# Eight single PSUM banks in one pool, freely placed steps, and a new order and buffer plan for an attention + gated-FFN kernel

## Chip, cores, metric

One core of a Trainium2 chip (the experiments ran on four chips; every ratio is to the kernel before on the same chip). The metric is the device time of one execution in microseconds (us). Most executions of one kernel agree to within 0.3%. Engines: PE does matrix products and PE transposes (PEld is its weight load), DVE, ACT and POOL do elementwise work, SP issues the DMA transfers from one queue, in program order.

## The reference, cut to what matters

```python
# q, k, v: (8 batches, 8 heads, 576, 64)
q_s = softmax(q, axis=-1); k_s = softmax(k, axis=2)
kv  = einsum('bhsd,bhse->bhde', k_s, v)              # 64 x 64 per head
x   = einsum('bhsd,bhde->bhse', q_s, kv)              # -> 4608 tokens x 512
out = ((x @ w1) * (x @ w2)) @ w3 @ w_out              # d_ff = 1024
```

In the course of the run 38.8 MB come in from memory: the weights and, batch by batch, q, k and v.

## The kernel before

The kernel is a list of about 1350 small steps. A step has an engine, dependencies and buffers. Three lists made by a search are stored in the file: `ORDER` (the order in which all steps are emitted), `SLOTS` (which tile of its pool each buffer takes) and, in `ORDER`, filler matmuls on a blank tile that keep PE busy while it would wait. A step waits for whatever last used the tile that it writes.

```python
tiles("st", 8, [P, 2 * RK * D], F32)      # staging tiles: every load lands in one of them
tiles("ps", 6, [P, 512], F32, psum)       # six single PSUM banks
tiles("pa", 1, [P, 2, 512], F32, psum)    # one double bank: all kv, x and query transposes of batch 0
...
def load(key, nbytes, rate, view, src):   # all loads, transposes and stores: one SP queue
    b = buf("st")
    def emit():
        nc.sync.dma_start(out=view(b.tile), in_=src)
...
def xm(...):                              # x product: four 64x64 quadrants side by side
    for j in range(2):
        for t in range(2):
            nc.tensor.matmul(px.tile[64*t:64*t+64, j, 0:n], lhsT=kv2..., rhs=qsT..., ...)
def xc(...):                              # its eviction, both banks in one ACT instruction
    nc.scalar.copy(out=xt_buf[g].tile[:, 2*i:2*i+2, o:o+n], in_=px.tile[:, :, 0:n])
...
for n in order:                           # emission
    if isinstance(n, tuple): self.fill(self.pools[n[0]][n[1]], n[2])
    else:                    self.tasks[n].emit()
```

Per batch: exponentials (ACT), sums (DVE), normalised queries (POOL), their transposes (by PE for batch 0, by DMA for the rest), kv, x. The FFN is computed in six token groups; five of them use a Winograd-like scheme with seven product pairs per block, evictions to `uu` tiles, sums from PSUM on DVE and a last product on POOL. W3·W_out is formed first, from eight w3 loads and four w_out loads.

The softmax here doesn't subtract the row's maximum and nothing guards it: scores larger than these inputs give would overflow.

Of the kernel before, what the change touches and what calls it, by code (L numbers as in the profile page):

```python
# [15 lines left out]

ORDER = [
    ('ps', 2, 27), 10, 6, 11, 4, 2, 8, 0, 142, 144, 96, 145, 97, ('ps', 2, 29), 151, 153, 152, 3, 98, 88,
    80, 143, 1, 81, 14, 89, ('ps', 2, 9), 104, 72, 90, 5, 73, ('ps', 2, 12), 17, 146, 154, 147, 7, 74, 12,
    82, 105, ('ps', 2, 3), 69, 148, ('ps', 2, 10), 16, 149, 15, 68, 150, 99, 70, 83, 128, 155, 91, 13, 106,  # L20
    100, 156, 92, 71, 101, 129, 84, 137, 75, 140, 136, 157, 76, 27, 159, 77, 158, 9, 102, 130, 21, 85, 103,
    141, 20, 131, 160, 138, 93, 86, 139, 132, 87, 161, 120, 107, 162, 94, 214, 112, 24, 163, 133, 164, 19,
    108, 212, 121, 182, 113, 213, 18, 165, 26, 78, 114, 166, 109, 79, 181, 167, 110, 168, 122, 95, 134, 22,
    169, 23, 193, 123, 170, 29, 124, 111, 28, 171, 176, 125, 135, 25, 126, 172, 32, 115, 127, 175, 116,
    427, 117, 205, 430, 207, 424, 431, 208, 436, 432, 428, 206, 437, 177, 425, 438, 179, 118, 187, 426,
    433, 188, 178, 173, 31, 439, 209, 429, 30, 210, 442, 119, 35, 440, 34, 443, 441, 454, 444, 215, 457,
    202, 434, 211, 189, 194, 445, 435, 455, 185, 446, 199, 216, 183, 451, 236, 190, 460, 184, 238, 461,
    447, 204, 448, 174, 456, 239, 449, 462, 463, 237, 36, 450, 203, 464, 37, 200, 458, 195, 466, 201, 217,
    33, 459, 452, 467, 465, 469, 192, 468, 219, 230, 220, 197, 218, 233, 1099, 221, 470, 186, 222, 180,
    1113, 223, 453, 38, 1106, 234, 232, 41, 196, 224, 1107, 231, 1114, 240, 198, 225, 235, 1092, 43, 191,  # L30
    1108, 250, 241, 251, 243, 1115, 245, 252, 1093, 471, 226, 1094, 244, 227, 242, 1109, 228, 269, 246,
    1100, 229, 1095, 270, 1101, 267, 40, 472, 1116, 39, 1110, 247, 1102, 473, 42, 1096, 248, 482, 268, 48,
    476, 1103, 491, 477, 475, 493, 506, 1117, 480, 507, 271, 478, 474, 481, 272, 253, 249, 492, 510, 479,
    483, 263, 494, 495, 521, 484, 508, 496, 485, 486, 254, 47, 498, 487, 266, 488, 511, 44, 255, 509, 499,
    497, 273, 489, 256, 513, 501, 500, 490, 522, 512, 502, 514, 503, 525, 264, 265, 504, 527, 516, 515,
    526, 523, 261, 536, 517, 505, 528, 524, 262, 518, 551, 529, 519, 553, 46, 274, 281, 530, 520, 1105,
    282, 537, 275, 45, 552, 538, 49, 276, 540, 539, 555, 1118, 541, 533, 283, 556, 531, 1104, 534, 543, 52,
    257, 554, 544, 566, 535, 1112, 542, 277, 258, 558, 567, 300, 568, 545, 546, 559, 570, 304, 532, 548,
    547, 259, 571, 561, 549, 260, 557, 581, 550, 560, 298, 573, 1120, 278, 562, 582, 279, 563, 302, 569,
    284, 583, 564, 574, 585, 572, 586, 1121, 575, 285, 576, 296, 587, 565, 577, 280, 578, 297, 588, 303,  # L40
    286, 301, 1127, 589, 584, 287, 1128, 305, 591, 50, 288, 1134, 1119, 579, 289, 1135, 299, 1111, 306,
    590, 580, 316, 1097, 327, 592, 593, 53, 307, 328, 317, 1148, 311, 318, 1149, 594, 290, 1129, 291, 595,
    1122, 308, 309, 1150, 335, 310, 292, 1136, 293, 1130, 312, 1098, 1123, 1131, 54, 596, 1141, 1124, 1137,
    598, 294, 1126, 600, 313, 295, 597, 1125, 314, 1142, 333, 51, 615, 601, 334, 1143, 616, 617, 1138, 319,
    618, 619, 320, 315, 1144, 599, 620, 602, 331, 329, 336, 604, 622, 330, 603, 61, 621, 623, 55, 1151,
    605, 60, 624, 321, 625, 1152, 56, 337, 607, 58, 1145, 338, 626, 630, 1140, 608, 627, 631, 606, 628,
    342, 632, 647, 322, 629, 633, 634, 340, 609, 610, 635, 363, 323, 343, 651, 324, 645, 611, 612, 646,
    637, 613, 660, 638, 341, 325, 614, 636, 661, 649, 326, 639, 640, 332, 648, 347, 650, 642, 366, 641, 59,
    664, 364, 643, 1139, 652, 348, 1146, 365, 653, 339, 662, 665, 362, 654, 675, 359, 655, 663, 676, 667,
    644, 656, 657, 668, 344, 666, 349, 358, 345, 677, 658, 361, 679, 57, 669, 670, 360, 63, 690, 678, 680,  # L50
    378, 671, 659, 691, 346, 672, 367, 682, 681, 683, 673, 692, 1153, 684, 379, 674, 65, 694, 380, 66, 705,
    695, 693, 64, 687, 1154, 685, 688, 1147, 350, 697, 686, 351, 689, 707, 698, 696, 706, 354, 699, 700,
    355, 709, 708, 702, 710, 720, 739, 404, 712, 703, 740, 724, 721, 704, 711, 713, 1155, 725, 714, 715,
    402, 701, 743, 1156, 722, 744, 717, 373, 728, 718, 371, 352, 746, 716, 719, 729, 1157, 62, 368, 353,
    726, 372, 67, 741, 1133, 369, 727, 356, 731, 742, 730, 732, 754, 747, 733, 745, 755, 370, 734, 723,
    1158, 748, 758, 1159, 736, 735, 759, 751, 374, 389, 749, 769, 391, 752, 1169, 770, 375, 750, 753, 1170,
    357, 1171, 737, 773, 395, 738, 760, 381, 761, 396, 382, 1162, 393, 392, 756, 390, 1163, 757, 376, 1172,
    762, 383, 771, 763, 384, 764, 405, 774, 1164, 1173, 394, 766, 772, 377, 776, 397, 765, 775, 777, 398,
    1165, 784, 1160, 1166, 767, 409, 1132, 785, 778, 779, 1175, 768, 790, 1174, 403, 788, 781, 789, 410,
    786, 411, 791, 780, 1183, 792, 787, 1184, 1176, 793, 799, 399, 1177, 406, 782, 400, 800, 796, 1185,  # L60
    385, 803, 1178, 804, 794, 401, 1186, 795, 1179, 1187, 797, 814, 806, 1188, 815, 798, 816, 1161, 386,
    801, 1189, 807, 805, 407, 1180, 818, 808, 387, 1182, 819, 1190, 817, 811, 388, 802, 809, 783, 408,
    1191, 810, 1192, 1193, 812, 821, 1168, 820, 822, 412, 829, 823, 413, 824, 1197, 830, 825, 835, 1194,
    826, 1196, 833, 827, 1195, 1198, 1181, 418, 828, 1204, 419, 1205, 834, 844, 831, 813, 836, 832, 1199,
    837, 845, 1200, 1206, 838, 1201, 848, 846, 1207, 841, 847, 1208, 839, 842, 849, 1209, 850, 414, 843,
    863, 851, 415, 852, 840, 864, 1211, 853, 865, 416, 867, 866, 1212, 868, 855, 854, 856, 1213, 857, 878,
    1214, 860, 1215, 870, 861, 1217, 858, 871, 869, 1203, 859, 879, 1225, 1210, 893, 872, 1202, 1218, 1167,
    882, 1216, 875, 883, 873, 876, 894, 1226, 874, 885, 877, 897, 1227, 898, 862, 880, 1219, 881, 900,
    1220, 901, 1228, 417, 884, 886, 899, 1229, 903, 902, 1221, 1230, 887, 888, 1222, 908, 904, 890, 889,
    905, 923, 891, 910, 906, 909, 895, 1232, 924, 896, 1233, 911, 1234, 907, 912, 1239, 913, 892, 420,  # L70
    1235, 915, 914, 916, 1240, 421, 917, 927, 1236, 1241, 928, 920, 422, 1242, 921, 918, 922, 930, 919,
    938, 931, 925, 939, 933, 926, 1243, 929, 423, 942, 1244, 968, 940, 1238, 943, 932, 1246, 1231, 1247,
    934, 1237, 945, 941, 935, 953, 936, 1248, 954, 1249, 937, 946, 1253, 944, 1250, 955, 947, 948, 1251,
    957, 1224, 949, 972, 1245, 950, 958, 1254, 1252, 951, 960, 956, 959, 952, 961, 1260, 973, 962, 1261,
    963, 970, 965, 964, 1255, 969, 1262, 966, 976, 987, 1263, 977, 971, 967, 988, 1256, 1264, 979, 978,
    974, 980, 1267, 1257, 981, 991, 1268, 1258, 992, 982, 1223, 994, 984, 983, 1269, 1259, 975, 985, 993,
    1265, 1002, 989, 986, 1270, 1003, 1266, 995, 1274, 996, 1271, 990, 1006, 1275, 1007, 1008, 997, 1009,
    999, 998, 1276, 1010, 1000, 1019, 1011, 1012, 1001, 1277, 1013, 1017, 1014, 1278, 1032, 1281, 1018,
    1033, 1282, 1020, 1015, 1036, 1004, 1021, 1283, 1005, 1022, 1037, 1284, 1016, 1024, 1023, 1285, 1038,
    1039, 1288, 1287, 1040, 1025, 1289, 1041, 1280, 1026, 1042, 1027, 1279, 1034, 1043, 1029, 1028, 1044,  # L80
    1286, 1049, 1290, 1045, 1030, 1064, 1035, 1291, 1031, 1062, 1047, 1046, 1292, 1295, 1048, 1296, 1293,
    1050, 1051, 1273, 1302, 1052, 1294, 1063, 1303, 1065, 1053, 1054, 1066, 1304, 1055, 1056, 1305, 1067,
    1057, 1059, 1306, 1297, 1058, 1060, 1069, 1307, 1298, 1308, 1068, 1077, 1299, 1309, 1078, 1316, 1301,
# [81 lines left out]
def kernel(  # L165
# [11 lines left out]
    nc = tc.nc  # L177
# [524 lines left out]
```

## Time and profile before

| | before |
|---|---|
| median | 243.96 us (3 runs, 242.98 to 244.15) |
| PE / DVE / ACT / POOL busy in the profiled run | 228.0 / 155.7 / 146.2 / 96.0 us |
| first W3·W_out product starts | 18.95 us |
| last matmul ends, then tail | 238.7 us, 4.6 us |
| filler matmuls | 90 |

The page of the kernel before: busy time of each engine, then PE's busy tenths in 40 slices of the span, the clock that the throttle granted PE, and the DMA engines' share.

```profile
PE 228.0 (94%) x1876; PEld 114.5 (47%) x1876; DVE 155.7 (64%) x293; ACT 146.2 (60%) x280; POOL 96.0 (39%) x85
...
PE   8897889988799999999989999999999999999992
...
PEclk9999999999999999999999999999999999999999
DMA  6999999999999999998995906272151004244656
```

The table of windows has one stretch per line: busy time (and number of instructions) of PE, PEld, DVE, ACT, POOL, then the mean granted clock, the DMA share (as the profile counts it, it can exceed 1) and the GB/s moved.

```profile
10.00:20.00 10.00, 8.39 (x87) 6.29 (x85) 7.23 (x13) 2.09 (x2) 2.14 (x1) 1.00 1.00 357
20.00:30.00 10.00, 7.83 (x81) 3.61 (x79) 4.84 (x7) 2.42 (x4) 5.84 (x4) 1.00 0.96 348
60.00:70.00 10.00, 8.30 (x115) 3.79 (x115) 6.59 (x15) 5.89 (x11) 5.04 (x4) 1.00 1.14 321
...
90.00:100.00 10.00, 9.81 (x126) 4.22 (x124) 6.81 (x15) 7.69 (x16) 6.37 (x5) 1.00 1.20 278
100.00:110.00 10.00, 10.00 (x55) 4.16 (x54) 7.58 (x14) 9.58 (x18) 6.29 (x5) 1.00 1.08 364
...
130.00:230.00 100.00, 100.00 (x623) 48.42 (x621) 62.20 (x116) 54.83 (x112) 33.34 (x29) 1.00 0.39 84
```

So the kernel has three stages: a start that waits for weights, a long middle in which PE runs just behind the loads (the DMA share stays near 1 to 120 us), and from 130 us a stretch in which PE is never idle. What PE does inside "busy" needs the timeline (start, duration, engine, line, operation, tiles, count). This is a stretch of the last stage:

```profile
170.96 0.59 PE L550 MATMUL ps<-xt,wc 128*128 128x512 f16 x2
171.39 0.59 PE L550 MATMUL ps<-xt,w 128*128 128x512 f16 x2
171.91 0.28 PE L466 MATMUL pa<-qsT,kv 64*64 64x192 f16 x4
172.12 0.60 PE L550 MATMUL ps<-xt,w 128*128 128x512 f16 x2
```

A pair of 512-column matmuls starts every 0.43 us. From the pair at 171.39 to the one at 172.12 it is 0.73 us although the x product between them needs only about 0.08: the visit to the 64x64 products costs about 0.22 us more. It is no single case: of the 51 visits in this trace 42 have no recorded idle time of PE in them, and the median of their extra time is 0.22 us. The Trainium skill, "TensorEngine Tiling (Array Packing)", Key Properties, states that a change of tiling mode drains the TensorE; this trace agrees with it, and gives the size of the whole visit (it cannot tell a drain from the weight loads of the four quadrants).

### The profile page before, as it was taken

To read this page: it belongs to the slowest core of one execution; us is meant where nothing else is said; L and a number is where in the kernel's file an instruction comes from. 1 tells how busy PE (TensorE), PEld (TensorE's weight loads), DVE (VectorE), ACT (ScalarE), POOL (GpSimd) and SP (SyncE) were. 2 spreads that over 40 slices of the span, in tenths; PEclk is the share of its full clock that TensorE was granted. 3 is DMA by queue.
4 is the path that set the end of the run, shared out by engine and by line. 5 is a ranking of instruction groups with operands and counts; after the bars stand their busy time and mean duration, and the time that the engine had idled before them with its cause. 6 is when DMAs were issued, how large, how long until landed. Compare 5 with 4: busy or idle time off the path is not lost.

```text
span 243.3 us, 4956 instructions
## 1 busy us (share of the span) xinstructions
PE 228.0 (94%) x1876; PEld 114.5 (47%) x1876; DVE 155.7 (64%) x293; ACT 146.2 (60%) x280; POOL 96.0 (39%) x85
## 2 busy tenths in 40 slices
PE   8897889988799999999989999999999999999992
PEld 5673344434346654444434444444444444566650
DVE  1474435889588985778978977467664566654330
ACT  4310486886499988998759785455645453444430
POOL 2033510235648566574834492454103312312020
PEclk9999999999999999999999999999999999999999
DMA  6999999999999999998995906272151004244656
GB/s 228 399 355 347 340 363 358 377 390 252 282 376 288 339 392 300 313 334 286 247 290 202 239 20 137 51 154 65 24 113 40 1 22 108 45 108 89 139 117 134
DMA packets 41879, 52.68 MB, mean 217 GB/s; under 512 B 18816, under 2 KB 22912, under 8 KB 41856
## 3 DMA queue, kind: packets, MB, share of 16 engines
q1 hardware_dynamic: 41856, 52.37, 74.7%
q8 instruction: 14, 0.23, 0.4%
q14 instruction: 9, 0.07, 0.1%
HBM read 38.80 MB, written 9.44 MB: 198 GB/s over the span
## 4 chain that ended last, share of the span: by engine, by line
PE 56%; DMA 25%; ACT 6%; DVE 4%; POOL 3%; issue 2%; SPq 2%; ACTq 0%; DVEq 0%; POOLq 0%
PE ps L550 32%; PE ps L616 22%; DMA qsT<-eq 9%; DMA st<-in_q_dram 6%; DMA st<-in_moe_w_dram 4%; DMA st<-in_k_dram 3%; DMA st<-in_moe_w_out_dram 3%; POOL eq L390 3%; SPq L233 2%; PE pa L466 2%; ACT uu L571 2%; ACT eq L376 1%; ACT ek L355 1%; DVE cc L574 1%; ACT osb L626 1%
## 5 line engine op out<-in xcount | busy, mean ns | idle before, releaser
L574 DVE TENSOR_TENSOR cc<-ps,uu 128x512 f16<-128x512 f32 (+2 forms) x120 | 66.9, 577 | 36.9 <-PE ps L550 16.8
L571 ACT COPY uu<-ps 128x512 f32<-128x512 f32 (+2 forms) x120 | 57.3, 505 | 38.8 <-PE ps L550 34.9
L616 PE MATMUL ps<-W3O,ab 128*128 128x512 f16 x288 | 76.2, 380 | 0.0
L601 POOL TENSOR_TENSOR ab<-cc,cc 128x512 f16<-128x512 f16 (+2 forms) x40 | 39.1, 982 | 76.6 <-DVE cc L574 76.0
L550 PE MATMUL ps<-tt,wc 128*128 128x512 f16 (+2 forms) x240 | 56.6, 337 | 0.1
L390 POOL TENSOR_TENSOR eq<-eq,ds 128x1152 f16<-128x1152 f16 x16 | 34.8, 2173 | 34.8 <-DVE ds L387 16.7
L550 PEld LDWEIGHTS <-wc 128*128 128x128 f16 x320 | 29.5, 98 | 28.9 <-DVE tt L529 0.7
L550 PE MATMUL ps<-xt,w 128*128 128x512 f16 (+2 forms) x160 | 38.6, 337 | 0.3
L616 PEld LDWEIGHTS <-ab 128*128 128x128 f16 x288 | 26.6, 98 | 25.7
L380 DVE TENSOR_REDUCE ds<-eq 128x9 f32<-128x576 f16 x32 | 23.5, 744 | 16.5 <-ACT eq L376 16.4
L550 PEld LDWEIGHTS <-w 128*128 128x128 f16 x240 | 22.2, 98 | 20.0 <-issue 0.8
L355 ACT ACTIVATE ek<-st 128x576 f16<-128x576 f32 x32 | 20.6, 688 | 14.8 <-DMA st<-in_k_dram 14.8
L626 ACT ACTIVATE osb<-ps 128x512 f32<-128x512 f32 x35 | 20.7, 603 | 14.3 <-PE ps L616 13.5
L376 ACT ACTIVATE eq<-st 128x576 f16<-128x576 f32 x32 | 21.3, 686 | 11.5 <-DMA st<-in_q_dram 10.2
L574 DVE TENSOR_TENSOR ab<-ps,cc 128x512 f16<-128x512 f32 (+2 forms) x40 | 22.8, 576 | 6.6 <-PE ps L550 5.5
L473 ACT CAST xt<-pa 128x512 f16<-128x512 f32 (+4 forms) x38 | 21.5, 565 | 6.3 <-PE pa L466 6.1
L365 POOL CAST v<-st 128x1152 f16<-128x1152 f32 x16 | 19.0, 1190 | 14.0 <-DMA st<-in_v_dram 9.6
L550 PE MATMUL ps<-xt,wc 128*128 128x512 f16 (+2 forms) x80 | 20.3, 337 | 0.0
L550 PE MATMUL ps<-tt,w 128*128 128x512 f16 (+2 forms) x80 | 19.9, 337 | 0.0
L309 PE MATMUL ps<-ab,ab 128*128 128x512 f16 x64 | 16.2, 380 | 0.7 <-DVE ab L276 0.3
L494 PE MATMUL ps<-xt,w 128*128 128x512 f16 x64 | 14.8, 379 | 0.9 <-ACT cc L501 0.9
L668 PE MATMUL ps<-blank 128*128 128x256 f16 x90 | 13.6, 317 | 1.1 <-DVE blank L660 1.1
(41 smaller groups left out, 136.4 us busy)
## 6 DMA issues: line engine op xcount, KB each, us to landing
st<-in_q_dram SPq DMA_DIRECT2D x16, 576.0 KB, 6.7
st<-in_v_dram SPq DMA_DIRECT2D x16, 576.0 KB, 6.8
st<-in_k_dram SPq DMA_DIRECT2D x16, 576.0 KB, 8.1
out_dram<-osb SPq DMA_DIRECT2D x72, 128.0 KB, 2.4
st<-in_moe_w_dram SPq DMA_DIRECT2D x16, 512.0 KB, 7.4
st<-in_moe_w_out_dram SPq DMA_DIRECT2D x4, 512.0 KB, 6.8
qsT<-eq SPq DMA_TRANSPOSE x14, 5.8
```

The source lines that it names most:

```text
L355: nc.scalar.activation(out=ek.tile[:, :, j, :], func=AF.Exp, in_=vk(bk.tile)[:, j].rearrange("p (r d) -> p r d", r=RK))
L365: nc.gpsimd.tensor_copy(out=v16.tile[:, :, :, 0:D].rearrange("p r j d -> p j r d"), in_=vv(bv.tile).rearrange("p j (r d) -> p j r d", r=RK))
L376: nc.scalar.activation(out=eq.tile[:, :, j, :], func=AF.Exp, in_=vq(bq.tile)[:, j].rearrange("p (r d) -> p r d", r=RK))
L380: nc.vector.tensor_reduce(out=ds.tile[:, 0, j], axis=AX.X, op=ALU.add, in_=eq.tile[:, :, j, :])
L390: nc.gpsimd.tensor_tensor(out=eq.tile, in0=eq.tile, op=ALU.mult, in1=ds.tile[:, 1].rearrange("p j r -> p r j")[:, :, :, None].broadcast_to ...
L473: nc.scalar.copy(out=xt_buf[g].tile[:, 2 * i:2 * i + 2, o:o + n], in_=px.tile[:, :, 0:n])
L550: nc.tensor.matmul(ps.tile[:, 0:h], lhsT=lhs(c), rhs=rhs(c), start=first and c == 0, stop=c == 1, skip_group_check=not first)
L571: return lambda: nc.scalar.copy(out=dst.tile[:, 0:h], in_=src.tile[:, 0:h])
L574: return lambda: nc.vector.tensor_tensor(out=dst(), in0=ps.tile[:, 0:h], in1=other.tile[:, 0:h], op=op)
L601: nc.gpsimd.tensor_tensor(out=ab.tile[:, 0:h], in0=c11.tile[:, 0:h], in1=c21.tile[:, 0:h], op=ALU.mult)
L616: nc.tensor.matmul(po.tile, lhsT=ab_buf[(g, ft)].tile[:, tb * P:(tb + 1) * P], rhs=W3O[ft], start=(ft == 0), stop=(ft == N_FT - 1))
L626: nc.scalar.activation(out=osb.tile, in_=po.tile, func=AF.Copy, scale=ISC)
```

## The change

The intent: with all eight banks in one pool, the x and kv products no longer queue for the one double bank; they take two single banks each and are evicted by two smaller instructions. Steps that can run on either of two engines (evictions on ACT or DVE, casts on DVE, ACT or POOL, sums and products on DVE or POOL) get their engine from a new list, `ENGS`. `ORDER` and `SLOTS` are searched again with the new freedom and new transfer rates in the search's model. Cut to its core (the lists themselves are left out):

```diff
-    tiles("ps", 6, [P, 512], F32, psum)
-    tiles("pa", 1, [P, 2, 512], F32, psum)
+    tiles("ps", 8, [P, 512], F32, psum)
...
+            elif self.tasks[n].alts:
+                self.tasks[n].emit(engs[n])
...
-                px = buf("pa")
+                px = [buf("ps"), buf("ps")]
...
-                def xc(i=i, px=px, g=g, o=o, n=n):
-                    nc.scalar.copy(out=xt_buf[g].tile[:, 2 * i:2 * i + 2, o:o + n],
-                                   in_=px.tile[:, :, 0:n])
+                for j in range(2):
+                    def xc(e, i=i, j=j, px=px, g=g, o=o, n=n):
+                        cast(e, xt_buf[g].tile[:, 2 * i + j, o:o + n], px[j].tile[:, 0:n])
...
-        pa, kv2, rc = buf("pa"), buf("kv2_"), buf("rc")
+        pk, kv2, rc = [buf("ps"), buf("ps")], buf("kv2_"), buf("rc")
...
-        e1 = add("ACT", ("e1", g, fb), ev(s1, X), [x1], [X, s1], k="ps", n=h)
+        e1 = add("ACT", ("e1", g, fb), ev(s1, X), [x1], [X, s1], FROM_PS, n=h)
...
-        k5 = add("POOL", ("k5", g, fb), mul, [k1, k4], [c11, c21, ab], k="tt", n=h)
+        k5 = add("POOL", ("k5", g, fb), mul, [k1, k4], [c11, c21, ab], dict(POOL="tt", DVE="tt16"), n=h)
...
 ORDER = [...]   SLOTS = [...]     # both replaced
+ENGS = {...}                      # engine of each free step
```

Against the old kernel, 107 of the new steps have moved engine: 72 evictions (67 of them from ACT to DVE), 20 sums and products and 15 casts. The order of the loads is new. There are 34 separate visits to the 64x64 products instead of 51, and 79 fillers instead of 90.

## The prediction

> **What bounds it now.** PE leads the busy times (228.0 of 243.3 us), but in three stages. (1) 0 to 20 us: the first loads. The timeline shows 90 filler matmuls on a blank tile (13.6 us in the groups); the first W3·W_out product starts at 18.95 us. (2) 20 to about 130 us: PE runs close behind the loads. The slices show DMA at 9 or more until then, and the chain of waits names query loads and transposes (DMA 25% of the span); PE still idles 1.0 to 2.2 us in each ten-us window from 10 to 70 us but that at 40. (3) From 130 to 234 us every window is PE 10.00: pairs of 512-column matmuls follow each other every 0.43 us, which is the array's rate. The tail after the last matmul is 4.6 us.
>
> Inside "busy", each visit to the 64x64 products (kv and x, four quadrants side by side) costs PE a switch. Around 171.4 us of the timeline a pair of matmuls to the start of the work after a 192-column x takes 0.73 us; 0.43 for the pair and 0.08 for the four quadrants leave about 0.22 us. The Trainium skill, "TensorEngine Tiling (Array Packing)", Key Properties, says that changing the tiling mode drains the TensorE; this trace agrees and puts about 0.22 us on it. There are 51 separate visits: about 11 us.
>
> **What the change does.**
> - One pool of 8 banks in place of 6 plus one double bank. The double bank carried every kv product, its normalisation and every x product one after another, so two x steps could not stand side by side without waiting for a 0.59 us eviction. The new order has 34 visits in place of 51: 17 x 0.22 = 3.7 us estimated. Perhaps 2.5 us of it is on the path.
> - Load order: w3 first, q later; the w_out half that the first product needs is eighth in place of ninth, so that product starts perhaps 2 us earlier. Fillers fall from 90 to 79. The w1/w2 loads come two places earlier. With the landings' measured spacing (1.28 us for w3 or w_out, 1.46 for w1/w2, 1.49 for q, k, v) in the new order, plus the PE work left after each load, the worst case is some 4 us better than for the old order.
> - Costs: x evictions become 76 of half the size (a 128x256 eviction takes 372 ns, a 128x512 one 587), kv normalisations 16 in place of 8. ACT falls from 146 to about 130 us, DVE rises from 156 to about 185 (30 uu and 21 x evictions and 16 k5 products move to it). POOL falls to about 86. DVE at almost 80% is the risk: it evicts the banks that PE needs, above all from 70 to 140 us.
>
> **Sum.** 2.5 us of switches, 3 to 4 us of start and load waits, little lost to DVE: 237.5 us, 80% range 233.5 to 242.5. Faster by over 2% (under 239.1): 0.66; within 2%: 0.30; slower: 0.04.
>
> **Right or wrong, in the profile.** First W3·W_out product near 17 us; PE's idle before it and up to 70 us about 3 us smaller; total of PE work from 130 us on at the array's rate still; last matmul about 4.6 us before the end. Wrong, if: PE waits for DVE between 70 and 140 us; loads land no earlier because staging buffers free later (casts moved to POOL at 1.04 us); or the saved switches all fall where PE waits for loads anyway.

## The result, and the profile after

The changed kernel is slower: median 253.33 us (4 runs, 251.81 to 254.11) against 244.06 us (4 runs, 242.98 to 244.84); ratio 1.0376 with a 95% interval of 1.0309 to 1.0443. A ratio here and below is the mean time of one kernel's runs over that of the other's of the same rounds, so it is not quite the ratio of the medians quoted. The mean granted clock was 0.975 to 0.980, against 0.998 in the profile of before.

The page and the windows of the changed kernel, columns as before:

```profile
PE 228.7 (91%) x1865; PEld 114.6 (46%) x1865; DVE 181.0 (72%) x375; ACT 132.2 (53%) x261; POOL 90.2 (36%) x76
...
PE   7885899989799986989998989999999999999992
...
PEclk9998999999979999799999999999999999999999
DMA  7987999999999999999989830670322200355357
```

```profile
10.00:20.00 10.00, 7.73 (x66) 5.44 (x63) 2.34 (x4) 3.41 (x5) 3.06 (x3) 1.00 0.92 308
20.00:30.00 10.00, 7.60 (x38) 3.42 (x39) 4.56 (x9) 1.05 (x1) 5.63 (x4) 0.83 0.86 307
...
70.00:80.00 10.00, 9.79 (x63) 5.76 (x62) 7.81 (x21) 8.22 (x20) 3.76 (x3) 0.83 1.06 353
...
90.00:100.00 10.00, 7.33 (x109) 3.44 (x107) 7.10 (x17) 5.75 (x11) 4.21 (x4) 1.00 1.15 259
100.00:110.00 10.00, 9.46 (x122) 3.89 (x123) 7.54 (x18) 5.71 (x14) 6.83 (x4) 0.83 0.95 284
...
130.00:230.00 100.00, 97.58 (x595) 45.72 (x594) 81.11 (x155) 45.01 (x92) 29.04 (x21) 1.00 0.42 89
```

Four things are to be seen. PE's busy time is the same to 0.7 us, so most of the 7.7 us of added span (251.0 against 243.3) is time in which PE stood idle; the matmuls at a halved clock hide in the busy time, which has 11 fewer fillers. DMA moved only 308 and 307 GB/s in the windows from 10 to 30 us, against 357 and 348. Three windows show a clock of 0.83; the trace has three stretches of half clock, 3.4 us each, from 22.74, 70.53 and 101.25 us. And in the last stage DVE is busy 81 of 100 us.

To place the loss, I counted at what time each kernel had done the same amount of useful PE work (every matmul at the rate of back-to-back pairs, 0.43 us for two of 512 columns; fillers left out; 200.1 us in all).

| useful PE work done, us | before reached it at | after | difference |
|---|---|---|---|
| 4 | 20.2 | 17.2 | -3.1 |
| 7 | 25.8 | 26.5 | +0.7 |
| 40 | 67.0 | 64.1 | -2.9 |
| 45 | 73.3 | 72.9 | -0.4 |
| 65 | 96.3 | 97.4 | +1.1 |
| 70 | 101.7 | 106.6 | +4.9 |
| 75 | 107.0 | 113.1 | +6.1 |
| 200.1 (end) | 238.7 | 246.0 | +7.4 |

The changed kernel began ahead, lost that lead by 26 us, was ahead again by 2.9 us at 64 us, as predicted, and lost it all, and more, by 113 us. Each of the three clock drops follows idle time of PE. In PE's timeline of the changed kernel, the value in brackets is PE's idle time just before the group, with what ended it:

```profile
14.85 1.02 PE L361 MATMUL ps<-ab,ab 128*128 128x512 f16 x4 [0.67 <-POOL ab L329]
17.59 0.82 PE L723 MATMUL ps<-blank 128*128 128x256 f16 x6
21.62 4.24 PE L361 MATMUL ps<-ab,ab 128*128 128x512 f16 x12 [3.21 <-DVE ab L329]
...
68.56 0.21 PE L482 MATMUL ps<-v,ek 64*64 64x65 f16 x1 [1.25 <-ACT ek L407]
...
94.72 0.25 PE L521 MATMUL ps<-qsT,kv 64*64 64x128 f16 x4 [1.18 <-DMA qsT<-eq]
...
100.54 0.44 PE L521 MATMUL ps<-qsT,kv 64*64 64x256 f16 x12 [1.88 <-DMA qsT<-eq]
100.92 0.75 PE L671 MATMUL ps<-W3O,ab 128*128 128x512 f16 x2
101.60 0.46 PE L521 MATMUL ps<-qsT,kv 64*64 64x256 f16 x4
101.99 2.74 PE L671 MATMUL ps<-W3O,ab 128*128 128x512 f16 x6
```

The first W3·W_out product came at 14.85 us, 4.1 us earlier than before; but then PE stood still for 3.21 us. What it waited for directly was the eviction of a transposed w3 tile on DVE (20.88 to 21.56 us); that stood in DVE's program order behind the cast of the third w_out tile, for which DVE itself had been idle 5.60 us, until the load landed at 19.59. The 12 matmuls from 21.62 took 4.24 us where the 0.43 us per pair gives 2.6, and the 6 from 101.99 took 2.74 where it gives 1.3: that is the halved clock.

### Where the loads were held

The SP queue issues in order, so a load that must wait for its staging tile holds everything behind it. Its timeline (SPq) in the changed kernel:

```profile
13.62 0.37 SPq L285 DMA_DIRECT2D st<-in_moe_w_out_dram  x1
14.04 1.97 SPq L285 DMA_DIRECT2D st<-in_moe_w_dram  x2
20.33 0.38 SPq L285 DMA_DIRECT2D st<-in_moe_w_out_dram  x1
20.81 0.41 SPq L285 DMA_DIRECT2D st<-in_v_dram  x1
```

Nothing was issued between 16.0 (14.04 + 1.97) and 20.33 us. The slot list and the trace together tell why. I worked out for each load which step had last read its tile, when that ended, and which other tiles no emitted step was still to read:

```
issued  load       tile  its last reader, end    other free tiles (since)
13.62   w_out(2)   7     cast w_out(1), 13.59    4 (5.2), 5 (7.8), 2 (12.0)
20.33   w_out(3)   7     cast w_out(2), 20.30    5 (7.8), 2 (12.0), 6 (14.8), 3 (15.8)
39.61   w2(2)      6     exp q(1,1),    39.59    0 (31.8), 5 (35.5)
```

The third and fourth loads of w_out go through the same tile 7, one after the other, while at least three other tiles lie free. The fourth cannot be issued before the third has landed (19.59) and been cast (20.30), although the queue had been ready since 16.0; w3(7) and two v loads that stood behind it had free tiles of their own. At 39.61 it is the same: the load before it was issued at 34.40, and for 4.8 us the queue waits for an exponential of a load that landed at 35.69, while tile 0 has been free since 31.8. Of 68 loads only 16 take the tile that has been free longest (23 in the kernel before). The load at 13.62 is of the same kind: it waited for tile 7, and tile 1 had not been used at all. The bytes that had landed by 40 and 60 us: 12.5 and 19.3 MB before, 12.0 and 18.7 MB after, so the lag is about one load.

The length of such stops does not tell the two kernels apart. Up to 60 us the queue issued nothing for over 1 us at a time nine times in the kernel before, 27.7 us in all, and eight times in the changed one, 29.9 us. What differs is that the DMA engines ran short in the changed kernel (shares of 0.92 and 0.86 between 10 and 30 us, against 1.00 and 0.96), and which loads were late.

That is a theory, though; the lag could as well come from the 107 moved steps (DVE 181 us busy), from the split banks, from the new order of the work itself, or from the clock alone.

### The profile page after: what moved, and what is told of

Same layout as the page of the kernel before. It is cut to its first block, busy times and chain, and to the rows that moved or that the text cites. A ratio compares the mean times of both kernels' runs of the same rounds, so it can differ in the third digit from the quotient of the medians.

```text
span 251.0 us, 4995 instructions
## 1 busy us (share of the span) xinstructions
PE 228.7 (91%) x1865; PEld 114.6 (46%) x1865; DVE 181.0 (72%) x375; ACT 132.2 (53%) x261; POOL 90.2 (36%) x76
## 5 line engine op out<-in xcount | busy, mean ns | idle before, releaser
L671 PE MATMUL ps<-W3O,ab 128*128 128x512 f16 x288 | 78.7, 385 | 0.2 <-DVE kv L498 0.2
L329 ACT COPY uu<-ps 128x512 f32<-128x512 f32 (+2 forms) x90 | 44.7, 515 | 48.5 <-PE ps L605 31.8
L656 POOL TENSOR_TENSOR ab<-cc,cc 128x512 f16<-128x512 f16 (+2 forms) x24 | 24.4, 1019 | 74.7 <-DVE cc L629 74.6
L605 PEld LDWEIGHTS <-wc 128*128 128x128 f16 x320 | 30.4, 99 | 34.6 <-issue 6.0
L605 PEld LDWEIGHTS <-w 128*128 128x128 f16 x240 | 23.2, 99 | 23.9 <-issue 1.4
L681 ACT ACTIVATE osb<-ps 128x512 f32<-128x512 f32 x29 | 17.1, 601 | 20.6 <-PE ps L671 14.4
L329 ACT CAST xt<-ps 128x256 f16<-128x256 f32 (+4 forms) x55 | 18.4, 375 | 9.6 <-PE ps L521 9.5
L329 POOL CAST v<-st 128x1152 f16<-128x1152 f32 x13 | 14.8, 1146 | 19.9 <-DMA st<-in_v_dram 19.2
L361 PE MATMUL ps<-ab,ab 128*128 128x512 f16 x64 | 17.5, 407 | 4.7 <-DVE ab L329 3.2
L605 PE MATMUL ps<-tt,w 128*128 128x512 f16 (+2 forms) x80 | 20.2, 336 | 0.0
L605 PE MATMUL ps<-xt,wc 128*128 128x512 f16 (+2 forms) x80 | 20.2, 341 | 0.0
L329 DVE COPY uu<-ps 128x512 f32<-128x512 f32 (+2 forms) x30 | 16.0, 537 | 4.8 <-PE ps L605 4.6
```

The source lines that it names most:

```text
L329: {"DVE": nc.vector.tensor_copy, "POOL": nc.gpsimd.tensor_copy, "ACT": nc.scalar.copy}[eng](out=o, in_=i)
L361: nc.tensor.matmul(pp.tile, lhsT=wT.tile[:, gt * P:(gt + 1) * P], rhs=wo[i][1].tile[:, (gt % 2) * C:(gt % 2 + 1) * C], start=(gt == 0), st ...
L605: nc.tensor.matmul(ps.tile[:, 0:h], lhsT=lhs(c), rhs=rhs(c), start=first and c == 0, stop=c == 1, skip_group_check=not first)
L656: {"POOL": nc.gpsimd, "DVE": nc.vector}[e].tensor_tensor(out=ab.tile[:, 0:h], in0=c11.tile[:, 0:h], in1=c21.tile[:, 0:h], op=ALU.mult)
L671: nc.tensor.matmul(po.tile, lhsT=ab_buf[(g, ft)].tile[:, tb * P:(tb + 1) * P], rhs=W3O[ft], start=(ft == 0), stop=(ft == N_FT - 1))
L681: nc.scalar.activation(out=osb.tile, in_=po.tile, func=AF.Copy, scale=ISC)
```

## Experiments

Theories. STAGING: the choice of staging tiles starves PE, and the clock drop follows. ENGINES: DVE, now busier, releases banks and casts late. STRUCTURE: the split banks and doubled evictions cost time. CLOCK: the idle stretches are harmless, but each throws the clock. CHAIN: the one late chain is the queries of batch 3. All kernels gave correct results. In what follows "old order" means the order, tiles and engines of the kernel before, put on the structure of the changed one.

| run | median us | ratio to before | 95% |
|---|---|---|---|
| 1 changed + fillers in the gaps | 253.07 | 1.0303 | 1.0234 to 1.0372 |
| 2 old order, 8 single banks | 244.73 | 0.9989 | 0.9951 to 1.0027 |
| 3 changed, old engines | 252.13 | none given (2 of 4 runs slow) | |
| 4 old order, new engines | 252.56 | 1.0303 | 1.0268 to 1.0337 |
| 5 old order, 14 visits merged away | 246.72 | 1.0096 | 1.0045 to 1.0148 |
| 6 changed, queries of batch 3 earlier | 253.56 | 1.0364 | 1.0311 to 1.0417 |
| 7 old order, new evictions only | 247.81 | 1.0120 | 1.0061 to 1.0178 |
| 8 old order, new sums and products only | 245.00 | 1.0007 | 0.9950 to 1.0064 |
| 9 changed, ten staging tiles, oldest first | 245.03 | 1.0036 | 0.9997 to 1.0074 |
| 10 old order, ten staging tiles, oldest first | 243.52 | 0.9961 | 0.9926 to 0.9996 |
| 11 run 9 with old engines | 245.46 | 1.0035 | 0.9996 to 1.0074 |
| 12 old order, new casts only | 247.65 | 1.0133 | 1.0089 to 1.0177 |
| 13 changed, eight staging tiles, oldest first | 246.57 | 1.0072 | 1.0043 to 1.0101 |
| 14 old order, eight staging tiles, oldest first | 243.48 | 0.9960 | 0.9930 to 0.9989 |
| 15 run 9 + fillers | 244.33 | 1.0005 | 0.9970 to 1.0040 |
| 16 changed, old casts | 251.25 | 1.0271 | 1.0238 to 1.0305 |
| 17 run 15, every pool oldest first | 243.50 | 0.9974 | 0.9944 to 1.0004 |
| 18 run 10, every pool oldest first | 243.63 | 0.9977 | 0.9941 to 1.0013 |

### 1. The clock alone

```diff
-('ps', 6, 6)                       # six fillers before the W3.W_out product that PE waited 3.21 us for
+('ps', 6, 32)
+14 before kv of batch 2, 9 and 15 before two x products of batch 3
```

> The kernel after, with 64 more filler matmuls where its PE sat idle: 26 more before the third w_out product (idle 18.4 to 21.6 us), 14 before the kv product of batch 2 (67.1 us), 9 and 15 before the two late x products of batch 3 (93.5 and 98.7 us). Theory CLOCK (the idle stretches halve PE's clock for 3.4 us each, three times, and this is a large part of the loss): the granted clock is 1.00 throughout and the time falls by 3 to 5 us, to 248.5 to 250.5 us. Rival LATE DATA (PE waits for the loads and transposes, the clock is only a consequence that is hidden): clock 1.00, but the time within 1 us of the kernel after, 252.5 to 254 us.

The profiled run had no drop and took 250.13 us at a mean clock of 0.997; the other three had 0.986 to 0.988 and took 252.59 to 253.71. The same kernel on the same chip thus lost about 3 us (mean 253.28, less 250.13) with the clock; the undisturbed side of this is a single execution. The windows from 66 to 74 us of the changed kernel and of this one show how the idle time turns into the drop:

```profile
66.00:70.00 4.00, 2.48 (x80) 1.48 (x79) 2.55 (x6) 3.65 (x8) 1.14 (x1) 1.00 1.26 238
70.00:74.00 4.00, 3.79 (x19) 1.75 (x18) 2.85 (x9) 3.13 (x7) 0.00 (x0) 0.57 1.05 386
```

```profile
66.00:70.00 4.00, 3.83 (x100) 2.76 (x98) 2.81 (x8) 3.37 (x9) 0.69 (x1) 1.00 1.03 225
70.00:74.00 4.00, 4.00 (x32) 2.60 (x31) 3.72 (x12) 3.79 (x10) 1.10 (x1) 1.00 1.04 398
```

PE busy 2.48 of 4 us in the changed kernel and 3.83 here (fillers included), then a clock of 0.57 and 1.00. The Trainium skill, "TensorE: Matmul & The Clock Gate", Part 1, has a table of two granted values, half and full, and names an idle window of about 3.4 us; its section on HAM oscillation states the rule as no idle gaps of PE above about 3.4 us. The drops here last 3.4 us and are to half, as it says. But none of the gaps ahead of them reached 3.4 us: 3.21 before the first, at most 1.25 before the second, 1.18 and 1.88 before the third. So shorter stops were enough. The clock records of the traces say more. Within each trace, all changes of the clock fall on one grid of 3.41 us, and where the grid lies against the kernel's start differs from run to run. Count PE's busy share in every such window of the 20 kept traces, from 12 us after the start to 8 us before the end: 1302 windows. In six PE was busy for less than 0.48 of the window, and after all six the clock was halved; in 15 for 0.48 to 0.59, and after three of them it was; after the other 1281 never. The windows before the three drops here were busy for 0.33, 0.49 and 0.45. So in these traces the busy share of a whole window tells more than the length of a gap, and the same stops can fall into one window or be split over two. CLOCK explains about 3 us; even at full clock the kernel is 250.13, and the rest stays.

### 2, 3, 4. Structure, order and engines taken apart

Each kernel is made by swapping whole lists: run 2 has all three old lists on the new structure, run 3 the old `ENGS`, run 4 the old `ORDER` and `SLOTS`.

```diff
-ORDER, SLOTS, ENGS = new, new, new
+ORDER, SLOTS, ENGS = old, old, old      # run 2
+ORDER, SLOTS, ENGS = new, new, old      # run 3
+ORDER, SLOTS, ENGS = old, old, new      # run 4
```

> The order, engines and buffers of the kernel before, on the new structure: eight single banks, kv and x products in two banks each, evicted by two instructions. Theory SCHEDULE (the loss is in the new order and engine choice, not in the structure): within 1% of the kernel before, 242 to 246 us, clock 1.00. Rival STRUCTURE (twice the x evictions and kv normalisations, each with its fixed cost, is what costs): 248 us or more.

> The kernel after, order and buffers kept, but every step that may run on either of two engines put back on the engine it has in the kernel before. Theory ENGINES (DVE at 72% and its in-order queue, with the moved evictions and casts, delays the chain of batch 3): faster than the kernel after by 2% or more, 248 us or less. Rival ORDER (the order of loads and steps sets it): as slow as the kernel after or slower, 252 to 258 us, since the order was chosen together with these engines.

> The order and buffers of the kernel before on the new structure, with the engine choices of the kernel after: the fourth corner of the square. Theory ENGINES: slower than e2 by 2% or more. Rival ORDER: within 1.5% of e2. If the two matter only together, this one and e3 are both slower than either matched pair.

Run 2 is level with the kernel before (0.9989): STRUCTURE falls, in the old order. Run 3's two fast runs took 249.25 and 251.09 us at a clock of 0.996 to 0.998, its other two 253.18 and 256.6; so old engines do not restore the time. The fair comparison is with run 1's execution at full clock, 250.13 us in the same rounds: at equal clock these few executions show no gain from the old engines. Run 4 costs 3.0% at full clock; counted by useful PE work it is 2.4 us behind the kernel before at 65 us, 4.3 at 110 and 7.6 at the end, so it loses over the whole run, not only under the loads. So the new order with its tiles loses even with the old engines, and the new engines lose even in the old order: two losses that do not add up: 3.0% for the engines in the old order, and in run 3's fast runs 1.7 and 2.4% for the order with its tiles (mean of the kernel before in these rounds: 245.2 us).

### 5. What a saved visit is worth

In run 2's order, kv and x products that belong together were moved side by side (51 visits become 37), with nothing else changed but the tiles that this made necessary.

```diff
-..., x(b, i, 0), <work>, x(b, i, 5), ...
+..., <work>, x(b, i, 0), x(b, i, 5), ...
```

> The kernel of e2 (order and engines of before, single banks) with 14 of its 51 visits to the 64x64 products removed: the second x of a pair is put right behind the first where four banks are free, and five of the first kv products right in front of the second. Nothing else moves but the evictions that belong to them. Theory SWITCH (a visit costs PE about 0.2 us and in the stage from 130 us on this is on the path): 0.5 to 2.5 us faster than e2, ratio to the kernel before 0.985 to 0.997. Rival HIDDEN (the saved switches lie where PE waits for loads, or holding four banks makes other steps wait): within 0.3% of e2, or slower.

It is slower by 1.0%. In the trace, the time beyond the ideal at the kv and x products fell by about 1.7 us, as the 0.22 us per visit would have it (14 x 0.22 = 3.1 at most), but the same sum at the Winograd-like products rose from 6.4 to 10.3 us: steps that had filled each other's waits no longer do. Here a saved visit was not worth its price even taken alone.

### 6. The late queries of batch 3

PE's two longest waits between 90 and 101 us name transposed queries. Run 6 emits the sums, normalisation and transposes of batch 3's queries earlier (the normalisation of the first 95 steps earlier; the second transpose moves up by only 3 places in the queue, not by the 6 that the expectation says), with the first two filler insertions of run 1.

```diff
-..., <other work>, sums q(3,0), normalise q(3,0), transpose q(3,0), ...
+..., sums q(3,0), normalise q(3,0), transpose q(3,0), <other work>, ...     # the same for q(3,1)
```

> The kernel after with the first two of e1's filler groups (26 and 14 more), and the chain of batch 3's queries (sums, reciprocal, product on POOL) put right behind its exponentials instead of behind the steps of group 1, and its two transposes 8 and 6 places earlier in the queue. Theory CHAIN (the x products of batch 3 came 7 to 10 us later than in the kernel before because DVE and POOL, in order, held their chain back; that is the stall between 93 and 101 us): the transposes land 8 and 4 us or more earlier (near 84 and 94 us), PE does not idle there, the clock stays at 1.00 from 94 to 110 us, and the time falls by 2 to 4 us against e1's run at full clock (250.1 us). Rival LOAD (DVE has too much work: taking the chain first delays the evictions as much): time within 1 us of e1's 250.1 us or worse.

The transposes landed at 84.1 and 97.0 us instead of 94.7 and 100.5, and the time did not move (1.0364). PE now waited for other work, 1.58 us before 76.5 for DVE and 1.54 us before 105.5 for an exponential, and the clock fell at 11.2, 76.0 and 106.8 us. CHAIN falls: bringing one chain forward only shows the next one that is late. After this the question was why the loads as a whole were behind.

### 7, 8, 12, 16. Which of the moved steps matter

Run 7 moves only the 72 evictions in the old order, run 8 only the 20 sums and products, run 12 only the 15 casts; run 16 is the changed kernel with its 15 casts put back. Example lines of `ENGS`, by name:

```diff
-e1(2,2): ACT     +e1(2,2): DVE           # run 7
-tt4(2):  DVE     +tt4(2):  POOL          # run 8
-w_out cast 0: DVE  +w_out cast 0: POOL   # run 12, and the reverse in run 16
```

> e2 with the new engine only for the 72 steps that evict a PSUM bank (mostly ACT to DVE). e4 with all 107 moved steps was 3% slower than e2. Theory EVICT (DVE with the moved evictions is too late for the steps behind it): at least 1.5% slower than e2. Rival SBUF (the moves of t sums and k5 products between POOL and DVE, or of the casts, cost it): within 0.7% of e2.

> e2 with the new engine only for the 20 steps of the second kind: 4 t sums from DVE to POOL (2.1 us there, 0.7 on DVE for 1024 columns) and 16 k5 products from POOL to DVE. Theory SBUF: at least 1% slower than e2, with PE idle before the first x2 or v2 of a group. Rival EVICT: within 0.7% of e2.

> e2 with the new engine only for the 15 casts (w3, w_out, w1, w2 casts and three v casts). e4 (all 107 moved) lost 3.0%, the evictions alone 1.2%, sums and products 0.1%. If the parts add up: this one loses 1.5 to 2% against e2. If the parts act only together (each engine has room for its own share, not for all): within 0.6% of e2.

> The kernel after with the 15 moved casts (7 of them to POOL, where 1024 columns take 1.04 us against 0.69 on DVE) back on their old engines. Theory CAST (casts on POOL free the staging buffers late): at least half of e9's gain, 249 us or less. Rival (the choice or number of buffers, whatever engine casts): 250.5 to 254 us.

Evictions cost 1.2% in the old order (three runs; one at 254.22 us and a clock of 0.982 left out), casts 1.3%, sums and products nothing. Together 2.6 of run 4's 3.0 points. By useful PE work the casts lose 2.7 us before 125 us and nothing after it, the evictions 0.3 us up to 110 us and 2.6 by the end. Put back in the changed kernel, the casts are worth about 1 point (1.0376 to 1.0271), and part of that is the clock, 0.988 to 0.997 in run 16. So ENGINES is not empty, but no part of it is the main thing. The casts read staging tiles, so they may act through the queue as well; that is argued, not shown.

### 9, 10, 11. More staging tiles

The changed kernel, with ten staging tiles given out anew: each load takes the tile that has been free longest. Nothing else differs. Runs 10 and 11 do the same to the old order and to run 3.

```diff
-    tiles("st", 8, [P, 2 * RK * D], F32)
+    tiles("st", 10, [P, 2 * RK * D], F32)
-SLOTS of the 68 loads: as searched
+SLOTS of the 68 loads: the free tile with the oldest last reader
```

> The kernel after with ten staging buffers for the loads in place of eight (the staging slots given out anew, least recently used first; nothing else changed). Theory STAGING (the new order frees staging buffers late, so that by 60 us only 18.7 MB of loads have landed against 20.5 MB in e2, and every later batch is late by that): 20 MB or more landed by 60 us, PE idle from 90 to 105 us mostly gone, 248 to 250.5 us. Rival QUEUE (the loads are late because they stand behind transposes in one in-order queue, or the evictions are late): less than 1.5 us faster than the kernel after.

> e2 with ten staging buffers. Its DMA engines are already at a share of 1.0 or more from 10 to 90 us, so the theory of a saturated DMA says: within 0.4% of e2 and of the kernel before. If staging buffers hold the loads back in this order too: 1 to 3 us faster, 242 to 243.5 us.

> e3 (order of after, engines of before) with ten staging buffers. If STAGING is what the order loses by, the two corrections together come to within 1% of the kernel before, 245 to 247.5 us at full clock; if the merged and late steps of the order itself (as e5 and e6 suggest) lose it: still 249 us or more at full clock.

Run 9 brings 1.0376 down to 1.0036. By 60 us 19.9 MB had landed (18.7 in the changed kernel; run 2's trace gives 19.9 too, not the 20.5 of the expectation), and at 40 us of PE work it is 6.8 us ahead of the kernel before. With the old engines (run 11, 1.0035) nothing changes any more. STAGING stands, and ENGINES no longer matters in the new order once the staging is mended. The old order gains as well, 0.4%.

### 13, 14. Number or choice?

Ten tiles change two things: how many there are, and which is taken. Run 13 keeps eight and changes only the choice (63 of 68 loads take another tile); run 14 does so in the old order.

```diff
     tiles("st", 8, [P, 2 * RK * D], F32)
-SLOTS of the 68 loads: as searched
+SLOTS of the 68 loads: the free tile with the oldest last reader
```

> The kernel after with its eight staging buffers, but each load takes the free buffer whose last reader is longest past in the order of the program (63 of 68 loads get another buffer); nothing else changed. In the kernel after only 16 of 68 loads take that one; many take a buffer freed two to ten steps before. Theory CHOICE (a load behind a just finished reader waits for it in the in-order queue, and all loads behind it too): most of e9's gain, 245 to 247 us. Rival NUMBER (eight are too few for this order): 250 to 254 us.

> The same new choice of staging buffers, eight of them, for e2 (order and engines of before; 23 of 68 loads took the oldest one there). Theory CHOICE: as fast as e10, 0.992 to 0.999 of the kernel before. Rival NUMBER: as e2, 0.997 to 1.003.

Run 13 is at 1.0072: the choice alone takes away 3.0 of the 3.8 points. The SP queue's timeline of run 13, to be laid beside that of the changed kernel:

```profile
13.39 0.38 SPq L287 DMA_DIRECT2D st<-in_moe_w_out_dram  x1
14.66 0.38 SPq L287 DMA_DIRECT2D st<-in_v_dram  x1
15.91 0.34 SPq L287 DMA_DIRECT2D st<-in_moe_w_dram  x1
16.89 0.54 SPq L287 DMA_DIRECT2D st<-in_v_dram  x1
17.61 0.37 SPq L287 DMA_DIRECT2D st<-in_moe_w_dram  x1
19.78 2.70 SPq L287 DMA_DIRECT2D st<-in_k_dram  x2
```

The last w_out load is issued at 13.39 us instead of 20.33 (and landed at 22.95 instead of 25.36), and in the time in which the changed kernel's queue stood still, between 16.0 and 20.3, three loads went out (16.89, 17.61, 19.78). The windows from 10 to 30 us carried 398 and 387 GB/s, against 308 and 307. Order and engines are the same in both kernels, and only loads write the staging tiles, so the same loads can be compared by name: the first k load of batch 0 landed at 30.3 us instead of 32.7, the first v load of batch 2 at 58.6 instead of 61.8, the second transposed query tile of batch 3 at 94.5 instead of 100.5. The stops of the queue before 60 us fell from 29.9 to 19.8 us. PE's waits shrank with it, from 3.21, 1.18 and 1.88 us to 1.57, 0.16 and 0.50:

```profile
21.07 2.76 PE L363 MATMUL ps<-ab,ab 128*128 128x512 f16 x12 [1.57 <-DVE ab L331]
90.13 0.25 PE L523 MATMUL ps<-qsT,kv 64*64 64x128 f16 x4 [0.16 <-DMA qsT<-eq]
94.58 0.44 PE L523 MATMUL ps<-qsT,kv 64*64 64x256 f16 x12 [0.50 <-DMA qsT<-eq]
```

In the old order the stops fell too, from 25.8 us in run 2 to 19.9 in run 14, but the time is only 0.4% under that of the kernel before. Run 13's clock still drops twice (mean 0.984 to 0.985 in all four runs).

### 15, 17, 18. What is left

Run 15 adds fillers to run 9 where PE still waits (14 before kv of batch 2, 6 and 16 before two x products of batch 3); run 17 gives out every pool's tiles oldest first as well; run 18 is that on run 10.

```diff
 # run 9
+('ps', .., 14) before kv(2,0);  ('ps', .., 6) before x(3,0,7);  ('ps', .., 16) before x(3,1,3)
+SLOTS of all pools: the free tile with the oldest last user      # run 17
```

> e9 with three groups of filler matmuls (14 before the kv product of batch 2, 6 and 16 before two x products of batch 3), where its profile has PE idle and the clock halved at 66.7 and 97.4 us. If the clock is what is left: clock above 0.995 in all runs and 1.5 to 3 us faster than e9, 242.5 to 243.7 us, below the kernel before. If the waits themselves are what is left: within 1 us of e9's 245.0 us.

> e15 (order and engines of after, ten staging buffers, fillers) with every pool's buffers, PSUM banks included, given out oldest first. If the choice matters in the other pools as in staging: 1 to 3 us faster than e15's 244.3 us, below the kernel before by 0.5% or more. If only the in-order load queue is sensitive to it: within 0.5% of e15.

> e10 (order and engines of before, ten staging buffers) with every pool given out oldest first. Same readings: 0.985 to 0.993 of the kernel before if the choice matters in other pools, 0.993 to 0.999 as e10 if not.

1.0036, 1.0005, 0.9974: each step helps by about 0.3 points, which is as much as one comparison can resolve. Run 17 is level with the kernel before, 4% below the changed kernel, and no better than the old order with the same treatment (run 18). Why does the new order then bring nothing? In run 17 it is 6.7 us ahead of the kernel before at 40 us of PE work and 5.3 us at 65, but only 1.6 us at 70. PE's timeline there:

```profile
92.08 1.91 PE L725 MATMUL ps<-blank 128*128 128x256 f16 x16
94.37 0.44 PE L523 MATMUL ps<-qsT,kv 64*64 64x256 f16 x12 [0.38 <-DMA qsT<-eq]
```

Sixteen fillers and a wait, for the second transposed query tile of batch 3. It lands at 94.3 us, and in the kernel before at 94.0. The gain of the start is given back at one landing that the new order does not bring forward. That this tile alone decides it was not tested with the staging repaired; run 6 moved it only in the starved kernel.

No run beats both kernels by more than the 2% that counts as a difference. The best are runs 10 and 14, the old order with staging tiles taken oldest first: 0.4% faster than the kernel before, the interval just clear of 1.

## Why the prediction was wrong, point by point

- **"the worst case is some 4 us better than for the old order"** is the step that failed. It summed landing spacings in the new order as if the queue never stood still. The queue did: 4.3 us at one load, 4.8 us at another. Instead of 4 us ahead, the loads were 0.5 MB behind at 40 us, and those of batch 3 came late: its last query load landed at 79.3 us (74.4 in the kernel before), its transposed queries at 94.7 and 100.5 (84.4 and 94.0). With the choice of tiles mended and nothing else (run 13) these came at 75.9, 90.1 and 94.5, and 3.0 of the 3.8 points went. The prediction did name "staging buffers free later" as something that would make it wrong, but gave it too little weight, and looked for it in slower casts instead of in the slot list, where it could have been read: which step last reads the tile that a load takes, and how close before the load it stands.
- **"17 x 0.22 = 3.7 us ... perhaps 2.5 us of it is on the path"**: the size of a switch was right, the gain was not. Run 5 took 14 visits away and cost 1.0%.
- **The clock was not considered at all.** Three drops cost about 3 us, by run 1's one execution without a drop.
- **"PE waits for DVE between 70 and 140 us"** as the main risk: DVE rose to 181.0 us (185 predicted), but run 11 shows that with the staging repaired old and new engines are level. In the old order the moved evictions and casts cost 1.2 and 1.3%.
- **"First W3·W_out product near 17 us"**: it came at 14.85, even earlier, and was followed at once by a 3.21 us stop.
- Right: ACT 132.2 us (130 predicted), POOL 90.2 (86), the tail 5.0 us (4.6), and that the structure itself does not cost (run 2). PE from 130 us on was not quite at its rate: busy 97.58 of 100 us.

The chance of 0.04 for "slower" was far too small for a change that replaced a whole tuned schedule.

What stays open: how much each single held load costs (the choice was changed for all 68 at once); why the stops cost the new order so much more than the old one (10.1 us of stops and 3.0 points less in run 13 than in the changed kernel, 5.9 us and 0.3 points less in run 14 than in run 2); why some windows in which PE is busy for about half halve the clock and others do not; and whether the landing at 94 us is all that keeps run 17 from being faster.

## What to carry to other kernels

In a queue that issues in order, give each load the buffer that has been free longest, and list for every load which step it waits for and how shortly before that step stands: one load that waits holds all the rest, and here that was 3.0 of 3.8% in the new order and 0.4% in the old. Two idle stretches of a microsecond or so within one window of 3.4 us can halve PE's clock for the next, so read the granted clock by windows before explaining a loss, and fill such gaps. A saved mode switch, or an engine with room, is worth nothing if the steps that move must then wait for each other.

## What the Trainium skill lacked or had wrong

- "TensorE: Matmul & The Clock Gate", HAM oscillation, gives the rule as no PE-idle gaps above about 3.4 us. Here the clock halved after gaps of at most 1.25 us (PE busy 2.48 of the 4 us before) and of 1.18 and 1.88 us (busy 4.78 of 8 us). The page's next section, on a second failure mode, does tell of short, frequent idle times that make the clock go up and down, but gives no measure; here it was the busy share of a window of 3.41 us: below 0.48 always, at 0.48 to 0.59 three times in 15, above never in 1281.
- "TensorEngine Tiling (Array Packing)", Key Properties, says that a mode switch drains the TensorE but gives no size: about 0.22 us per visit (42 visits, median) to 64x64 products between 128x128 products in the trace of the kernel before.
- No page that I looked up warns that the choice of staging tile alone can hold an in-order issuing queue: 1.0376 to 1.0072 by the choice (run 13), 4.3 and 4.8 us without an issue at two loads.
- "GPSIMD Engine Reference", section 3.1, has a two-tensor sum of fp32 at 1.96 times DVE's time. For fp16 it has no figure; here a sum of 128x1024 took 2.13 us on POOL and 0.68 to 0.96 us on DVE, 2.2 to 3.1 times, as three of the groups of the changed kernel show (line, engine, operation, tiles, shape, count, busy us, mean ns, idle before).

```profile
L584 DVE TENSOR_TENSOR tt<-xt 128x1024 f16<-128x1024 f16 x5 | 4.8, 961 | 0.4 <-ACT xt L329 0.3
L584 DVE TENSOR_TENSOR tt<-tt,xt 128x1024 f16<-128x1024 f16 x3 | 2.1, 686 | 0.1
L584 POOL TENSOR_TENSOR tt<-xt,tt 128x1024 f16<-128x1024 f16 x2 | 4.3, 2127 | 3.2 <-DVE tt L584 3.2
```
